# Five gate blocks per batch with one matmul less, the mirror made by ScalarE, VectorE and POOL

## The chip, the cores and the metric

The kernel runs on one core of one Trainium2 chip. The time is the device time of the core in microseconds (us), the median of several executions. A ratio between two kernels is the mean time of the one's fast runs over the mean time of the other's fast runs of the same rounds, so it is not quite the ratio of the medians that stand beside it. A verdict of "faster" or "slower" needs a difference of 2%. Engines: PE is TensorE (PEld its weight load), DVE is VectorE, ACT is ScalarE, POOL is GpSimd, SP issues DMAs.

## The reference

```python
X = np.fft.fft(x, axis=1); X = np.fft.fft(X, axis=2)   # x: 8 x 3008 x 256
y = X.real.reshape(24064, 256)
g = y @ w_gate                                          # 256 x 1536
val = y @ w_val                                         # 256 x 1536
out = (gelu(g) * val) @ w_out                           # 1536 x 256, gelu with erf
```

The DFT's real part has a symmetry. The kernel splits each row into an even part E and an odd part O. A row's gate is `X = E·Wg + O·Wg`, and the gate of its mirror row is `E·Wg − O·Wg` (plus a correction, `EB * yw`, because partition 0 of the odd half carries a row that does not change its sign). So one block of work makes two sets of up to 512 rows.

## The kernel before

The batch is cut into 3 chunks of 512, 512 and 481 columns, each into 12 blocks of 128 features: 36 blocks a batch, numbered 0 to 35 here, 288 in all. One block is the work of one (chunk, fc) pair, woven with the previous block's second half and with the second matmul (L2) of the previous chunk. `# ...` marks what is left out.

```python
        def l1_gate(ci, fc):
            def run():
                n, _, E, O, st, fs = cols_of(ci, fc)
                pg = psum("g")                                     # two banks
                mm(pg, n, "g", "E", fs, E, True, False)
                mm(pg, n, "g", "O", fs, O, False, True)
                gl = gelu_tile()
                nc.scalar.activation(gl[:, 0, :n], pg[:, :n], AF.Gelu)
                st["ps"][fc] = [pg, gl]
            return run

        def l1_gate2(ci, fc):                                      # one block later
            def run():
                n, _, _, O, st, fs = cols_of(ci, fc)
                pg, gl = st["ps"][fc][:2]
                mm(pg, n, "g", "M", fs, O, False, True, skip_group_check=True)   # adds -2 O: now E - O
                nc.scalar.activation(_sub(gl, [[-1, n]], TOK + n - 1), pg[:, :n], AF.Gelu)
            return run
        # ... l1_value: E into pv, ve = EB * yw + pv on DVE
        # ... l1_value2: O into pv; h0 = gelu * pv and vv = 2 ve - pv on DVE; h1 = gelu * vv on POOL

    def tp_rows(b, gi):            # after DFT row group gi: copies one row into EB and into partition 0 of EO
        def run():
            n, y = chunk_len[gi], yrow_dram[b % 2]
            o = y.offset + chunk_off[gi]
            nc.sync.dma_start(
                out=_sub(EB_bufs[b], [[1, n]], chunk_off[gi]), in_=ap_replace(y, ap=[[0, 128], [1, n]], offset=o))
            nc.sync.dma_start(
                out=_sub(EO_bufs[b], [[1, n]], HALF + chunk_off[gi], part_num=1),   # HALF = 1505
                in_=ap_replace(y, ap=[[0, 1], [1, n]], offset=o))
        return run
    # ...
        for i, (parts, fc) in enumerate(blocks):       # the order of one block
            parts["G"][fc]()                           # two gate matmuls, gelu
            if before: before[0]["g"][before[1]]()     # previous block: third gate matmul, mirror gelu
            parts["V"][fc]()                           # value, even
            # four L2 matmuls
            for f in pool.pop(i, []): f()              # POOL folds of a later batch
            if before: before[0]["v"][before[1]]()     # previous block: value, odd; products
            # four L2 matmuls
            for f in fill.pop(i, []): f()              # DFT of the next batch, loads, row copies
            before = parts, fc
```

The fill table holds the next batch's first DFT stage (`s1t`), its last stage (`tp_y`, `tp_e`, `tp_o`, evacuated into EO_sb by ACT), the loads of the batch after, and the row copies. An evacuation copies a finished PSUM bank into SBUF, which frees the bank; a fold is one of POOL's sums over the input rows of a later batch, made before its DFT.

## Time and profile before

| | before |
|---|---|
| median time | 630.39 us (629.39 to 630.58, 3 runs) |
| span of the profiled run | 627.0 us, granted clock 0.996 |
| PE busy | 612.3 us, 98% |
| DVE, ACT, POOL busy | 578.3, 428.4, 505.3 us |

From the page of the kernel before: busy time by engine, the granted TensorE clock in 40 slices (9 is 90% or more), the chain of work that ended last, and the group of gate matmuls (count, then busy us and mean ns of one, then idle time of the engine before them and what ended most of it).

```profile
PE 612.3 (98%) x4195; PEld 405.1 (65%) x4243; DVE 578.3 (92%) x941; ACT 428.4 (68%) x842; POOL 505.3 (81%) x510
...
PEclk8999999999999999999999999999999999999999
...
PE 93%; ACT 2%; issue 1%; DVE 1%; DMA 1%; POOL 1%; POOLq 0%; ACTq 0%
...
L660 PE MATMUL ps_g<-EO_sb,W_sb 128*128 128x512 bf16 (+1 forms) x817 | 228.5, 375 | 3.8 <-ACT gelu_sb L685 0.8
```

The timeline of TensorE in one block of the last batch, before. The columns are start and duration in us, engine, line, operation, tiles and forms, and how many instructions were merged.

```profile
551.41 0.81 PE L660 MATMUL ps_g<-EO_sb,W_sb 128*128 128x512 bf16 x2
552.06 0.38 PE L660 MATMUL ps_v<-EO_sb,W_sb 128*128 128x512 bf16 x1
552.27 0.60 PE L749 MATMUL ps_o<-Wo_sb,h_sb 128*128 128x256 bf16 x4
552.71 0.38 PE L660 MATMUL ps_v<-EO_sb,W_sb 128*128 128x512 bf16 x1
552.93 0.60 PE L749 MATMUL ps_o<-Wo_sb,h_sb 128*128 128x256 bf16 x4
553.36 0.38 PE L660 MATMUL ps_g<-EO_sb,W_sb 128*128 128x512 bf16 x1
```

From 551.41 to 553.36 is one block: 1.95 us. The distance of starts, not the duration, is a matmul's price: 552.27 − 552.06 = 0.21 us for 512 columns, although each matmul "takes" 0.38. (The third gate matmul's record is missing here: 0.65 us pass between 551.41 and 552.06, which is three matmuls.) So the kernel is bound by matmul columns, and a matmul removed is worth 0.2165 us if nothing else waits.

### The profile page before, as it was taken

Reading aid. Unit: us, or ns where it says so; the run is one execution under the profiler, and the core shown is the slowest. Engines: PE = TensorE matmul, PEld = TensorE weight load, DVE = VectorE, ACT = ScalarE, POOL = GpSimd, SP = SyncE. Lnnn points to the kernel's source line nnn. Section 1 sums busy time; section 2 is a strip of 40 time slices with the busy share of each in tenths; the row PEclk is TensorE's granted clock in tenths of the full one; section 3 lists DMA queues with packets and bytes.
Section 4 is the critical chain, followed back from the end, with each engine's and each line's share of the span. In section 5 each row is a group of like instructions: output and inputs, shape, how many; then the busy total and the mean of one; then the engine's idle time right before and its main releaser. Section 6 shows DMA issues by size and latency. Waiting matters only on the chain.

```text
span 627.0 us, 12895 instructions
## 1 busy us (share of the span) xinstructions
PE 612.3 (98%) x4195; PEld 405.1 (65%) x4243; DVE 578.3 (92%) x941; ACT 428.4 (68%) x842; POOL 505.3 (81%) x510
## 2 busy tenths in 40 slices
PE   7999999999999999999999999999999999999997
PEld 3456666666666666666666666666666666666666
DVE  8689989999899999999999998999999999999992
ACT  6777677666776677667676677676676666666661
POOL 8399999989897998879997899969988655555651
PEclk8999999999999999999999999999999999999999
DMA  9961754536353353731645335633212322221123
GB/s 177 227 97 31 210 129 116 144 105 159 99 146 101 98 133 79 184 113 46 160 110 135 101 78 127 148 97 98 62 49 63 91 86 55 51 52 39 42 51 81
DMA packets 54217, 65.40 MB, mean 104 GB/s; under 512 B 7831, under 2 KB 49802, under 8 KB 51754
## 3 DMA queue, kind: packets, MB, share of 16 engines
q1 hardware_dynamic: 47222, 49.03, 30.6%
q0 software_dynamic: 6608, 15.29, 11.4%
q8 instruction: 33, 0.54, 0.4%
q10 hardware_dynamic: 320, 0.26, 0.2%
q14 instruction: 34, 0.28, 0.2%
HBM read 39.65 MB, written 30.17 MB: 111 GB/s over the span
## 4 chain that ended last, share of the span: by engine, by line
PE 93%; ACT 2%; issue 1%; DVE 1%; DMA 1%; POOL 1%; POOLq 0%; ACTq 0%
PE ps_o L749 38%; PE ps_g L660 28%; PE ps_v L660 19%; PE ps_dft L546 2%; PE ps_dft L582 2%; PE ps_o L820 1%; DMA Z_sb<-z 1%; PE ps_dft L443 1%; PE ps_dft L612 0%; ACT gelu_sb L676 0%; POOL h_sb L724 0%; POOL eo_sb L224 0%; DMA out_dram<-out_sb 0%; ACT gelu_sb L685 0%; PE ps_dft L749 0%
## 5 line engine op out<-in xcount | busy, mean ns | idle before, releaser
L724 POOL TENSOR_TENSOR h_sb<-gelu_sb,v_sb 128x512 bf16<-128x512 bf16 (+1 forms) x280 | 319.8, 1146 | 93.1 <-DVE v_sb L722 85.9
L749 PE MATMUL ps_o<-Wo_sb,h_sb 128*128 128x256 bf16 (+1 forms) x2232 | 334.9, 273 | 0.9 <-POOL h_sb L724 0.9
L749 PEld LDWEIGHTS <-h_sb 128*128 128x128 bf16 (+1 forms) x2304 | 228.7, 100 | 112.9 <-POOL h_sb L724 2.6
L676 ACT ACTIVATE gelu_sb<-ps_g 128x512 bf16<-128x512 f32 (+1 forms) x288 | 169.4, 588 | 98.6 <-PE ps_g L660 80.9
L660 PE MATMUL ps_g<-EO_sb,W_sb 128*128 128x512 bf16 (+1 forms) x817 | 228.5, 375 | 3.8 <-ACT gelu_sb L685 0.8
L704 DVE SCALAR_TENSOR_TENSOR ve_sb<-EB_sb,yw,ps_v 128x512 f32<-128x512 bf16 (+1 forms) x280 | 206.3, 737 | 25.9 <-PE ps_v L660 25.0
L660 PE MATMUL ps_v<-EO_sb,W_sb 128*128 128x512 bf16 (+1 forms) x575 | 213.7, 375 | 0.7 <-DVE W_sb L451 0.6
L720 DVE TENSOR_TENSOR h_sb<-gelu_sb,ps_v 128x512 bf16<-128x512 bf16 (+1 forms) x280 | 189.9, 678 | 1.1 <-ACT gelu_sb L685 0.7
L660 PEld LDWEIGHTS <-W_sb 128*128 128x128 bf16 x1440 | 137.2, 98 | 81.1 <-issue 1.8
L722 DVE SCALAR_TENSOR_TENSOR v_sb<-ve_sb,ps_v 128x512 f32<-128x512 f32 (+1 forms) x280 | 187.5, 670 | 0.0
L685 ACT ACTIVATE gelu_sb<-ps_g 128x512 bf16<-128x512 f32 (+1 forms) x288 | 168.7, 586 | 0.0
L769 ACT ACTIVATE out_sb<-ps_o 128x512 f32<-128x512 f32 x92 | 55.0, 598 | 35.7 <-PE ps_o L749 35.6
L224 POOL TENSOR_TENSOR eo_sb<-ab_sb 94x512 bf16<-94x512 f32 (+1 forms) x70 | 77.6, 1111 | 0.5
L549 ACT ACTIVATE S_sb<-ps_dft 96x512 bf16<-96x512 f32 x56 | 32.9, 588 | 14.0 <-PE ps_dft L546 13.9
L592 ACT ACTIVATE EO_sb<-ps_dft 128x512 bf16<-128x512 f32 (+1 forms) x44 | 26.0, 590 | 23.3 <-PE ps_dft L582 22.1
L217 POOL TENSOR_TENSOR ab_sb<-x_raw,x_raw 94x508 f32<-94x508 f32 (+1 forms) x30 | 33.0, 1100 | 0.0
L220 POOL TENSOR_TENSOR ab_sb<-x_raw,x_raw 94x508 f32<-94x508 f32 (+1 forms) x30 | 32.9, 1098 | 0.0
L546 PE MATMUL ps_dft<-eo_sb,G 94*96 94x256 bf16 x119 | 22.5, 274 | 0.2 <-POOL eo_sb L224 0.2
L158 POOL DMA_INDIRECT x_raw<-in_x_dram,idx x18 | 17.1, 948 | 2.9 <-issue 1.1
L582 PE MATMUL ps_dft<-TP,Z_sb 128*128 128x128 bf16 (+1 forms) x184 | 17.8, 218 | 0.0
L582 PEld LDWEIGHTS <-Z_sb 128*128 128x128 bf16 x192 | 14.6, 98 | 1.8 <-DVE Z_sb L534 0.6
L546 PEld LDWEIGHTS <-G 94*96 94x96 bf16 x119 | 13.0, 123 | 1.2 <-issue 0.4
(148 smaller groups left out, 166.2 us busy)
## 6 DMA issues: line engine op xcount, KB each, us to landing
out_dram<-out_sb SPq DMA_DIRECT2D x364, 64.0 KB
x_raw<-in_x_dram SPq DMA_DIRECT2D x10, 768.0 KB
Z_sb<-z SPq DMA_DIRECT2D x7, 768.0 KB
z<-S_sb SPq DMA_DIRECT2D x7, 576.0 KB
EB_sb<-yrow SPq DMA_DIRECT2D x14, 128.0 KB
z<-S_sb SPq DMA_DIRECT2D x7, 192.0 KB
x_raw<-in_x_dram SPq DMA_DIRECT2D x2, 640.0 KB
EB_sb<-yrow SPq DMA_DIRECT2D x7, 120.2 KB
```

Source lines behind the costliest of these rows:

```text
L224: eng.tensor_tensor(_sub(eo, [[C, nj], [1, 128]], j0 * C + g * 128), ab(0, 0, [[1, 128]]), ab(1, 0, [[1, 128]]), op=op)
L546: nc.tensor.matmul(ps[:96, q * C : (q + 1) * C], G[:, j, :], _sub(eo, [[1, C]], j * C), start=(j == js[0]), stop=(j == js[-1]))
L582: nc.tensor.matmul(ps[:, o : o + n], st["Z"][:, pair, g * 128 : g * 128 + 128], _sub(TP, [[1, n]], g * 128), start=True, stop=True)
L660: nc.tensor.matmul(ps[:, :n], W[nm, part][:, fs], src, start=start, stop=stop, **kw)
L676: nc.scalar.activation(gl[:, 0, :n], pg[:, :n], AF.Gelu)
L685: nc.scalar.activation(_sub(gl, [[-1, n]], TOK + n - 1), pg[:, :n], AF.Gelu)
L704: nc.vector.scalar_tensor_tensor(ve[:, :n], EB_bufs[b][:, c0 : c0 + n], yw[:, fc : fc + 1], pv[:, :n], op0=ALU.mult, op1=ALU.add)
L720: nc.vector.tensor_tensor(st["h"][:, fc, 0, :n], gl[:, 0, :n], pv[:, :n], op=ALU.mult)
L722: nc.vector.scalar_tensor_tensor(_sub(vv, [[-1, n]], n - 1), ve[:, :n], 2.0, pv[:, :n], op0=ALU.mult, op1=ALU.subtract)
L724: nc.gpsimd.tensor_tensor(st["h"][:, fc, 1, :n], gl[:, 1, :n], vv[:, :n], op=ALU.mult)
L749: nc.tensor.matmul(pso[:m, half], st["h"][:, fc, sign, h0 : h0 + m], Wo_sb[:, fc, :], start=(fc == 0 and not (first and sign)), stop=(fc = ...
L769: nc.scalar.activation(_sub(osb, [[1, 2 * C]], 0, part_num=m), pso[:m, :], AF.Copy)
```

## The change

In blocks 4, 10, 21, 28 and 33 of batches 1 to 6 the third gate matmul goes. The mirror gate is made as `2E + EB*ywg − X` instead: ACT copies 2E out of the bank (e2) before the odd matmul is added, DVE forms `EB*ywg − X`, POOL adds e2. That is 30 matmuls less: 18 of 512 columns and 12 of 481, 6.3 us of TensorE. Two schedule changes go with it: POOL's folds are moved off the chunk ends, and the last DFT stage of batches 3 to 7 is packed into fewer blocks, earlier.

```diff
+    GATE2 = (4, 10, 21, 28, 33)
         def l1_gate(ci, fc):
+                if two_gate(ci, fc):
+                    mm(pg, n, "g", "E", fs, E, True, True)
+                    e2 = e2_tile()
+                    nc.scalar.activation(e2[:, :n], pg[:, :n], AF.Copy, scale=2.0)
+                    st["ps"][fc] = [pg, gelu_tile(), e2]
+                    return
+        def l1_gate_odd(ci, fc):                       # after the first four L2 matmuls
+                mm(pg, n, "g", "O", fs, O, False, True, skip_group_check=True)
+                nc.scalar.activation(gl[:, 0, :n], pg[:, :n], AF.Gelu)
+                d = v_tile()
+                nc.vector.scalar_tensor_tensor(
+                    d[:, :n], EB_bufs[b][:, c0 : c0 + n], ywg[:, fc : fc + 1], pg[:, :n],
+                    op0=ALU.mult, op1=ALU.subtract)
+                nc.gpsimd.tensor_tensor(d[:, :n], e2[:, :n], d[:, :n], op=ALU.add)
         def l1_gate2(ci, fc):                          # one block later, as before
+                if two_gate(ci, fc):
+                    nc.scalar.activation(_sub(gl, [[-1, n]], TOK + n - 1), pg[:, :n], AF.Gelu)   # pg is d here
+                    return
# ... (tiles, ywg made once at block 14, the call of "O" in the loop)
+                slot_of = [s + {NFC - 1: 2, 0: 1}.get(s % NFC, 0) for s in slot_of]          # folds
-            spread(b, items, s + 7, s0 + NS - 3)
+            spread(b, items, s + 7, s0 + NS - 10 if b > 2 else s0 + NS - 3)                   # DFT rows
```

More of the change, by code (lines that the diff above doesn't have):

```diff
@@ L135, in v_tile, with e2_tile @@
         return work([128, TOK], FP32, "v", 4, "v_sb")
+    def e2_tile():
+        return work([128, TOK], FP32, "e2", 1, "e2_sb")
     def osb_tile():
@@ L245 @@
     one_h = const_pool.tile([1, 1], BF16)
-    yw = const_pool.tile([128, NFC], FP32)
+    yw, ywg = (const_pool.tile([128, NFC], FP32, name=f"yw_{i}") for i in "vg")
     NGP = NJ * NK
@@ L477, in make_yw, with make_ywg @@
         return run
+    def make_ywg():
+        fcs = sorted({i % NFC for i in GATE2})
+        ps = psum("dft")
+        for fc in fcs:
+            nc.tensor.matmul(
+                ps[:, fc : fc + 1], W["g", "O"][0:1, fc * 128 : (fc + 1) * 128], one_h, start=True, stop=True)
+        for fc in fcs:
+            nc.scalar.activation(ywg[:, fc : fc + 1], ps[:, fc : fc + 1], AF.Copy, scale=2.0)
     EO_bufs, EB_bufs = {}, {}
@@ L634, in tp_o @@
         return tp_e(b, gi, 1, engine)
+    NS = NG * NFC
+    GATE2 = (4, 10, 21, 28, 33)
     def store(b, gi, sub, sign, osb_half, queue):
@@ L667, in cols_of, with two_gate @@
             return n, c0, E, O, cstate[ci], slice(fc * 128, (fc + 1) * 128)
+        def two_gate(ci, fc):
+            return 0 < b < B - 1 and ci * NFC + fc in GATE2
         def l1_gate(ci, fc):
@@ L678, in l1_gate, with run @@
             return run
+        def l1_gate_odd(ci, fc):
+            def run():
+                if not two_gate(ci, fc):
+                    return
+                n, c0, _, O, st, fs = cols_of(ci, fc)
+                pg, gl, e2 = st["ps"][fc][:3]
+                del st["ps"][fc][2]
+                mm(pg, n, "g", "O", fs, O, False, True, skip_group_check=True)
[5 more added lines that the diff above has]
+                nc.gpsimd.tensor_tensor(d[:, :n], e2[:, :n], d[:, :n], op=ALU.add)
+                st["ps"][fc][0] = d
+            return run
         def l1_gate2(ci, fc):
@@ L683, in run @@
                 pg, gl = st["ps"][fc][:2]
+                if two_gate(ci, fc):
+                    nc.scalar.activation(_sub(gl, [[-1, n]], TOK + n - 1), pg[:, :n], AF.Gelu)
+                    return
                 mm(pg, n, "g", "M", fs, O, False, True, skip_group_check=True)
@@ L777, in ffn_work @@
             parts = {k: [f(ci, fc) for fc in range(NFC)] for k, f in (
-                ("G", l1_gate), ("V", l1_value), ("g", l1_gate2), ("v", l1_value2))}
+                ("G", l1_gate), ("O", l1_gate_odd), ("V", l1_value), ("g", l1_gate2), ("v", l1_value2))}
             subs = [nsub - 1, *range(nsub - 1)] if last(ci) else range(nsub)
@@ L874, in behind_first_gate @@
         tp_y(0, 0)()
-    NS = NG * NFC
     def plan():
@@ L894, in plan @@
             at(fill, s, f)
+        at(fill, 14, make_ywg)
         for i, f in enumerate(early):
@@ L921, in plan @@
                 slot_of = [4, 4, 5, 5, 6, 6, 7, 7, 8, 8, 9, 13, 13, 14, 15, 15, 16, 17, 17, 18]
+            else:
+                slot_of = [s + {NFC - 1: 2, 0: 1}.get(s % NFC, 0) for s in slot_of]
             for s, f in zip(slot_of, ops):
@@ L972, in feed @@
                 two.pop(0)()
+            parts["O"][fc]()
             for f in pool.pop(i, []):
```

## The prediction

> **What bounds the kernel.** TensorE. The page has PE busy 98% of 627.0 us, and the chain of waits is 93% PE. The Trainium skill ("Perfetto Trace Analysis", Identifying the Most-Contended Engine) warns that matmul busy time says little, because matmuls are pipelined, so I took the pitch of matmul starts from the timeline: 0.2165 us for 512 columns, 0.2035 for 481, 0.109 for 256. One F block of 512 columns is 5 x 0.2165 + 8 x 0.109 = 1.954 us, the period seen in the last batch. A middle batch takes 73.9 us, and its column work with the DFT rows leaves under 1 us unexplained (missing matmul records are not stalls). VectorE is close behind: three instructions a block at about 0.60 each, so 1.8 to 1.85 of 1.954 us. ScalarE needs 2 x 0.49 us a block plus evacuations, POOL 1.12 us for the product plus folds of about 1.22.
>
> **What the change does.** In 5 of 36 blocks of batches 1 to 6 (30 blocks) it removes one gate matmul: 3 x 0.2165 + 2 x 0.2035 = 1.06 us a batch, 6.3 us in all. That is the ceiling. It adds per such block one ACT copy (0.49 to 0.60 us), one DVE instruction (about 0.60) and one POOL fp32 sum (about 1.23, like the fp32 folds).
>
> **What comes back as stalls.** The odd matmul accumulates onto the bank that ACT is still copying. From the start of the even matmul: data out about 0.48 us later, copy 0.60, ACT end to PE start 0.05 (seen where ps_o waits for its evacuation): 1.12 us. PE fills 3 x 0.2165 + 4 x 0.109 = 1.085 us meanwhile: a stall of 0.04. But two of the five blocks (local block 9 of chunks 1 and 2) begin just after an output evacuation on ACT, which puts the copy 0.2 us later: about 0.27 lost. In block 21 the moved DFT row (block 20) queues a second evacuation ahead: about 0.5 lost. Estimate: 3 x 0.04 + 0.27 + 0.5 = 0.9 us lost a batch, against 1.06 saved: PE ps_g waiting for ACT e2.
>
> The rest should be absorbed. DVE needs 7 x 0.6 = 4.2 us in two blocks that PE now does in 3.7; it lags 0.5 us and recovers in three or four blocks within three value banks. The mirror gelu waits for POOL's sum: it starts about 3.7 us after the block began, with room until 4.0, so only a fold just before costs about 0.1. "SBUF — State Buffer" (two separate sides) says a VectorE instruction with two SBUF inputs and a GpSimd one exclude each other; the new difference reads one operand from PSUM, so I expect no blocking.
>
> The moved folds and rows remove little: steady stalls were only about 0.2 us a batch (a gate waiting for its bank behind two evacuations). About -1 us for all. The extra ywg start costs 0.2 to 0.5.
>
> **Predicted: 628.0 us, 624.5 to 632.0 (8 in 10)**, ratio 0.996. Faster by over 2%: 0.01; within 2%: 0.96; slower by over 2%: 0.03.
>
> **What would show it.** L660 matmuls into ps_g fall by 30. PE waits on the ACT copy, most in blocks 21 and 33, near zero in 4, 10 and 28. DVE busy rises 18 to 22 us, ACT about 18, POOL about 36; PE still about 97%. A middle batch shortens by 0.1 to 0.6 us.
>
> **What would make it wrong.** If the copies start earlier than I read, the time nears 624. If POOL's sum is late (over 1.4 us, or behind folds), the mirror gelu blocks ACT in order, the gate banks come late, and the time exceeds 631.

## More of the kernel before

One line of the list of waits of before will matter later (engine, tile and line, what it waited for, total us, times, longest):

```profile
ACT EO_sb L592 <- DMA EO_sb<-yrow: 1.1, 2, 0.6
```

## The result, and the profile after

| | before | after |
|---|---|---|
| median time | 630.3 us (629.39 to 630.58, 4 runs: the three above and one more) | 679.29 us (679.19 to 680.5, 4 runs) |
| ratio | | 1.0784, 95% interval 1.0766 to 1.0803 |
| span, clock | 627.0 us, 0.996 | 677.3 us, 0.977 |

The change is 7.8% slower. The page of the kernel after, the same four lines:

```profile
PE 625.0 (92%) x4168; PEld 406.7 (60%) x4216; DVE 587.2 (87%) x971; ACT 448.3 (66%) x875; POOL 541.3 (80%) x540
...
PEclk9999999998979989999899998999999999999999
...
PE 8%; POOL 2%; DVE 1%; ACT 1%; issue 0%; SPq 0%; DMA 0%; POOLq 0%; ACTq 0%
...
L677 PE MATMUL ps_g<-EO_sb,W_sb 128*128 128x512 bf16 (+1 forms) x787 | 229.0, 381 | 23.2 <-ACT gelu_sb L731 18.3
```

The gate matmuls fell by 30, from 817 to 787 records, yet PE's busy time rose by 12.7 us, and the clock row shows 8s and 7s where it had 9s: for stretches the granted clock fell. The chain could not be followed back far this time (its shares add up to little), so it is not used. The list of waits after shows where engines stood; line numbers moved with the edit.

```profile
ACT gelu_sb L728 <- POOL v_sb L719: 34.9, 28, 4.2
...
DVE v_sb L716 <- ACT gelu_sb L714: 21.1, 30, 1.2
PE ps_g L677 <- ACT gelu_sb L731: 18.3, 17, 5.9
ACT EO_sb L605 <- DMA EO_sb<-yrow: 15.3, 3, 5.8
PE ps_o L795 <- ACT out_sb L815: 13.8, 15, 2.2
```

Two stories are in it. The first two lines belong to the new chain (L714 gelu, L716 difference, L719 sum, L728 mirror gelu); in the last, TensorE waits for an output evacuation, which ACT makes late when it stands in that chain. The fourth line is an old wait, 1.1 us before, now 15.3 us in three places, and it is not part of the gate at all: it is the evacuation of the last DFT stage into EO_sb waiting for a row copy. Most of the third line follows from it: 15.6 of the 18.3 us are three waits (4.81, 4.85 and 5.90 us) right behind those three evacuations.

To see where the 50 us arose, I took the length of the blocks in both traces (the distance between the `ve` instructions of neighbouring blocks on DVE; there are 280, the first eight blocks have none) and subtracted. Sums by batch, with blocks that differ by more than 0.9 us:

| batch | longer by, us | where |
|---|---|---|
| 1 | 8.6 | block 4 +1.25, 12 +1.19, 21 +1.31, 28 +0.95, 30 +3.79, 33 +1.04 |
| 2 | 13.8 | 4 +1.06, 6 +4.48, 10 +1.06, 21 +1.62, 27 +5.13, 28 +1.57 |
| 3 | 10.5 | 6 +1.19, 21 +1.54, 27 +5.15, 28 +1.75 |
| 4 | 11.4 | 6 +1.17, 21 +1.54, 27 +6.20, 28 +1.77 |
| 5 | 3.9 | 6 +1.17, 21 +1.54, 28 +0.93 |
| 6 | 3.3 | 21 +1.54, 28 +1.15, 33 +1.04 |

In batch 5, whose last x load is issued in block 7, and in batch 6, which has none, the gate blocks and their neighbours alone cost. The big steps at block 27 come in batches 2 to 4 alone. Here is block 27 of batch 4 in the timeline of after: the row copy is issued, and the evacuation behind it starts 8.3 us later.

```profile
409.80 0.34 SPq L641 DMA_DIRECT2D EO_sb<-yrow  x1
...
418.13 0.57 ACT L605 ACTIVATE EO_sb<-ps_dft 128x481 bf16<-128x481 f32 x1 [5.82 <-DMA EO_sb<-yrow]
418.60 0.57 ACT L702 ACTIVATE gelu_sb<-ps_g 128x481 bf16<-128x481 f32 x1
...
419.68 0.96 PE L677 MATMUL ps_g<-EO_sb,W_sb 128*128 128x481 bf16 x2 [5.90 <-ACT gelu_sb L731]
```

ACT works in order: while it waits for the copy it makes no gelu, so no gate bank comes free, and TensorE stands for 5.90 us. The stretches around it, after (columns: the stretch and its length, then busy us of PE, PEld, DVE, ACT, POOL with instruction counts, then granted clock, DMA share, GB/s):

```profile
405.00:413.00 8.00, 8.00 (x63) 5.31 (x61) 7.65 (x13) 5.64 (x12) 7.65 (x8) 1.00 0.61 141
413.00:419.60 6.60, 0.78 (x7) 0.47 (x5) 1.67 (x3) 1.47 (x3) 3.24 (x4) 0.86 0.75 168
419.60:424.00 4.40, 4.32 (x16) 2.48 (x16) 1.71 (x3) 1.64 (x4) 1.30 (x2) 0.50 0.11 29
424.00:428.00 4.00, 4.00 (x27) 2.62 (x26) 3.63 (x7) 3.61 (x7) 4.00 (x4) 0.93 0.05 11
```

After the wait TensorE is "busy" but makes 16 matmuls in 4.40 us, against 27 in the next 4.00: the clock is 0.50. So a wait like this one is paid for a second time. It is also the larger part of the rise of PE's busy time: in the five half-clock stretches before the run's end PE was busy 24.7 us, and about half of that, 12.3 us, is extra (an estimate from the trace); what else made PE busier was not traced. The Trainium skill ("TensorE: Matmul & The Clock Gate", What's actually happening) says the array falls to half clock after an idle window of about 3.4 us and returns after a busy one; this trace agrees on the two values of the clock, and its half-clock stretches are 3.41 or 6.83 us long, one or two such windows (but for the last, which the run's end cuts). On the word idle, see the last section.

The other half of the story is one gate block, block 10 of batch 4, after. Read it as a chain: copy, odd matmul (second PE line), gelu, difference, sum, mirror gelu.

```profile
375.07 0.60 PE L677 MATMUL ps_g<-EO_sb,W_sb 128*128 128x512 bf16 x2
375.49 0.60 ACT L696 ACTIVATE e_sb<-ps_g 128x512 f32<-128x512 f32 x1 [0.59 <-PE ps_g L677]
...
376.16 0.38 PE L677 MATMUL ps_g<-EO_sb,W_sb 128*128 128x512 bf16 x1
...
376.64 0.60 ACT L714 ACTIVATE gelu_sb<-ps_g 128x512 bf16<-128x512 f32 x1
...
377.27 0.75 DVE L716 SCALAR_TENSOR_TENSOR v_sb<-EB_sb,yw_g,ps_g 128x512 f32<-128x512 bf16 x1 [0.41 <-ACT gelu_sb L714]
...
378.09 1.27 POOL L719 TENSOR_TENSOR v_sb<-e_sb,v_sb 128x512 f32<-128x512 f32 x1 [0.59 <-DVE v_sb L716]
...
379.40 0.63 ACT L728 ACTIVATE gelu_sb<-v_sb 128x512 bf16<-128x512 f32 x1 [0.86 <-POOL v_sb L719]
...
379.94 0.58 ACT L815 ACTIVATE out_sb<-ps_o 97x512 f32<-97x512 f32 x1
```

The copy costs TensorE nothing here: the odd matmul follows at 376.16, 1.09 us after the even one, as the prediction had it. But the difference does not start when the matmul is done. It waits for the gelu, which reads the same PSUM bank, and starts at 377.27. The mirror gelu therefore starts 379.40 − 375.07 = 4.33 us after the first matmul, not 3.7, and ACT was idle for 0.86 us before it. Behind it in ACT's queue stands the output evacuation (379.94), which frees the only ps_o bank.

### The profile page after: what moved, and what is told of

Its sections match the earlier page's. It is cut to its first block, busy times and chain, and to the rows that moved or that the text cites. A ratio compares the mean times of both kernels' runs of the same rounds, so it can differ in the third digit from the quotient of the medians.

```text
span 677.3 us, 12863 instructions
## 1 busy us (share of the span) xinstructions
PE 625.0 (92%) x4168; PEld 406.7 (60%) x4216; DVE 587.2 (87%) x971; ACT 448.3 (66%) x875; POOL 541.3 (80%) x540
## 3 DMA queue, kind: packets, MB, share of 16 engines
q0 software_dynamic: 6608, 15.29, 10.5%
## 5 line engine op out<-in xcount | busy, mean ns | idle before, releaser
L795 PE MATMUL ps_o<-Wo_sb,h_sb 128*128 128x256 bf16 (+1 forms) x2232 | 340.1, 276 | 14.6 <-ACT out_sb L815 13.8
L795 PEld LDWEIGHTS <-h_sb 128*128 128x128 bf16 (+1 forms) x2304 | 231.2, 101 | 137.4 <-issue 25.9
L677 PE MATMUL ps_g<-EO_sb,W_sb 128*128 128x512 bf16 (+1 forms) x787 | 229.0, 381 | 23.2 <-ACT gelu_sb L731 18.3
L750 DVE SCALAR_TENSOR_TENSOR ve_sb<-EB_sb,yw_v,ps_v 128x512 f32<-128x512 bf16 (+1 forms) x280 | 205.6, 734 | 36.1 <-PE ps_v L677 35.5
L677 PE MATMUL ps_v<-EO_sb,W_sb 128*128 128x512 bf16 (+1 forms) x575 | 216.6, 380 | 1.4 <-DVE W_sb L454 0.6
L702 ACT ACTIVATE gelu_sb<-ps_g 128x512 bf16<-128x512 f32 (+1 forms) x258 | 151.8, 588 | 86.4 <-PE ps_g L677 58.4
L677 PEld LDWEIGHTS <-W_sb 128*128 128x128 bf16 x1410 | 135.3, 98 | 101.4 <-issue 28.8
L731 ACT ACTIVATE gelu_sb<-ps_g 128x512 bf16<-128x512 f32 (+1 forms) x258 | 151.4, 587 | 0.0
L719 POOL TENSOR_TENSOR v_sb<-e_sb,v_sb 128x512 f32<-128x512 f32 (+1 forms) x30 | 37.4, 1246 | 23.0 <-DVE v_sb L716 23.0
L605 ACT ACTIVATE EO_sb<-ps_dft 128x512 bf16<-128x512 f32 (+1 forms) x44 | 25.8, 587 | 27.9 <-DMA EO_sb<-yrow 15.3
L728 ACT ACTIVATE gelu_sb<-v_sb 128x512 bf16<-128x512 f32 (+1 forms) x30 | 18.6, 619 | 34.9 <-POOL v_sb L719 34.9
L716 DVE SCALAR_TENSOR_TENSOR v_sb<-EB_sb,yw_g,ps_g 128x512 f32<-128x512 bf16 (+1 forms) x30 | 22.1, 736 | 21.1 <-ACT gelu_sb L714 21.1
L696 ACT ACTIVATE e_sb<-ps_g 128x512 f32<-128x512 f32 (+1 forms) x30 | 17.6, 587 | 9.4 <-PE ps_g L677 9.4
```

Of the source, the lines that this page charges most:

```text
L677: nc.tensor.matmul(ps[:, :n], W[nm, part][:, fs], src, start=start, stop=stop, **kw)
L719: nc.gpsimd.tensor_tensor(d[:, :n], e2[:, :n], d[:, :n], op=ALU.add)
L750: nc.vector.scalar_tensor_tensor(ve[:, :n], EB_bufs[b][:, c0 : c0 + n], yw[:, fc : fc + 1], pv[:, :n], op0=ALU.mult, op1=ALU.add)
L795: nc.tensor.matmul(pso[:m, half], st["h"][:, fc, sign, h0 : h0 + m], Wo_sb[:, fc, :], start=(fc == 0 and not (first and sign)), stop=(fc = ...
```

## The experiments

Thirteen kernels ran; all gave correct results. Each set was timed against the kernel before on its own chip.

Theory A: two separate causes. (1) The gate chain ends later than predicted, and ACT, in order, holds back the evacuation and the next gate bank. (2) The packed DFT rows bring an evacuation behind a row copy that lands late. Theory B: the schedule is harmless and everything comes from the gate blocks. Theory C (for the gate alone): VectorE has no room for 30 more instructions.

### e1_schedule_only

```diff
-    GATE2 = (4, 10, 21, 28, 33)
+    GATE2 = ()                      # and no ywg; folds and rows as in the change
```

> The moved folds and the earlier rows, with no two-pass block. Theory A (the loss has two separate parts: the chain copy - odd matmul - gelu - difference - sum - mirror gelu in 30 blocks, and the evacuation of the last DFT row, which waits for the row copy that now lands late behind the x loads): 642 to 648 us, with the waits of ScalarE's EO_sb for the EO_sb<-yrow copy still about 15 us in three places. Theory B (the schedule alone is harmless; all comes from the two-pass blocks): 629 to 631 us.

Measured: 659.04 us (654.12 to 659.6) against 629.81, ratio 1.0438 (1.0393 to 1.0483). Theory B is out. Theory A had the kind right and the size too small: 29 us, not 12 to 18. Its list of waits has

```profile
ACT EO_sb L605 <- DMA EO_sb<-yrow: 18.8, 4, 6.1
```

and around the one of batch 2 (stretches, columns as above)

```profile
234.50:241.50 7.00, 2.05 (x16) 1.26 (x14) 2.76 (x5) 0.85 (x2) 4.35 (x5) 0.96 0.90 211
241.50:247.80 6.30, 5.03 (x18) 2.74 (x18) 1.94 (x3) 2.85 (x6) 2.85 (x3) 0.50 0.07 21
```

so the half clock comes on top: blocks 27 and 28 of batch 2 are together 8.6 us longer (6.96 + 1.64) for a wait of at most 6.1. Batches 5 and 6 are 0.10 and 0.13 us longer: with the same packed rows, but no x load near the row copies, there is no cost.

### e2_rows_back

```diff
-            spread(b, items, s + 7, s0 + NS - 10 if b > 2 else s0 + NS - 3)
+            spread(b, items, s + 7, s0 + NS - 3)
```

> The change with the DFT rows spread as before (up to NS - 3), folds still moved, two-pass blocks kept. Theory A: about 17 us less than the changed kernel, 659 to 665 us, and the waits of EO_sb for EO_sb<-yrow under 2 us. Theory B: 676 us or more.

Measured: 660.01 us (658.34 to 661.59), ratio 1.0488 (1.0465 to 1.0511). As theory A has it: 19 us go with one number. (Packed rows with the folds in their old place were not run. The blocks of the x loads hang on those of the folds, but they hardly moved: the loads ahead of the late copy are issued in blocks 24 and 25 in both kernels.)

### e3_gates_only

```diff
-                slot_of = [s + {NFC - 1: 2, 0: 1}.get(s % NFC, 0) for s in slot_of]
+                pass                # folds as before; rows as before too
```

> The two-pass blocks alone: folds and rows where they were before. Theory A: 630 + 6 x 3.3 us, plus a few us where POOL's sum comes late behind folds: 650 to 657 us. Theory B: 675 us or more. If the folds moved off the chunk ends help the two-pass blocks, this one is slower than e2_rows_back; if they hurt (bunched folds delay POOL's sum), it is faster.

Measured: 653.43 us (651.95 to 655.38), ratio 1.0372 (1.0339 to 1.0404). The gate blocks alone cost about 24 us. What is left of TensorE's waits for the output evacuation is

```profile
PE ps_o L795 <- ACT out_sb L815: 9.1, 16, 2.2
```

The gate blocks are 7 us faster with the folds where they were (e2): the moved folds are bunched, and POOL's sum waits in the queue behind them. In e2 block 30 of batch 1 and block 6 of batch 2 are 3.15 and 3.85 us longer than before, in e3 0.85 and 2.51. A part of that is again the half clock: after the start e2 has two such stretches of 3.41 us, e3 one.

### e4_rows_padded

Everything in the change stays, but the odd half of EO_sb starts at an even element.

```diff
-        return work([128, 2, HALF], BF16, "EO", 2, "EO_sb")
+        return work([128, 2, 1536], BF16, "EO", 2, "EO_sb")
-            dst = _sub(EO_bufs[b], [[1, n]], g * HALF + chunk_off[gi])
+            dst = _sub(EO_bufs[b], [[1, n]], g * 1536 + chunk_off[gi])
-                out=_sub(EO_bufs[b], [[1, n]], HALF + chunk_off[gi], part_num=1),
+                out=_sub(EO_bufs[b], [[1, n]], 1536 + chunk_off[gi], part_num=1),
```

> The changed kernel whole, but the odd half of EO_sb begins at element 1536 instead of 1505, so that a row copy and the next evacuation no longer touch neighbouring odd elements; the 14 waits of EO_sb evacuations for a DMA are gone from the program, and nothing else moves. Theory A: the three waits of 5 to 6 us at block 27 of batches 2 to 4 vanish, 660 to 665 us. If it is the late landing itself that holds the kernel, or the row copies' traffic, it stays at 677 us or more.

Measured: 661.22 us (658.16 to 661.84), ratio 1.0488 (1.0453 to 1.0523). So the wait did not protect anything the program needed: the row copy of the first chunk ends at element 2016, counted from the tile's start, the next evacuation begins at 2017, and with 1505 as the start of the half each such pair was ordered. With 1536 the next chunk begins at an even element (2048), the 14 waits (two a batch) are gone from the trace, and 18 us from the time. (That the ordering is by a unit larger than one 2-byte element is an inference from this; which unit was not tried.)

The next three separate the parts of the gate chain.

### e5_difference_first

Two-pass blocks alone, as e3, with the two readers of the bank in the other order.

```diff
                 mm(pg, n, "g", "O", fs, O, False, True, skip_group_check=True)
-                nc.scalar.activation(gl[:, 0, :n], pg[:, :n], AF.Gelu)
                 d = v_tile()
                 nc.vector.scalar_tensor_tensor(d[:, :n], ..., pg[:, :n], ...)
+                nc.scalar.activation(gl[:, 0, :n], pg[:, :n], AF.Gelu)
                 nc.gpsimd.tensor_tensor(d[:, :n], e2[:, :n], d[:, :n], op=ALU.add)
```

> Two-pass blocks alone (as e3_gates_only), but the VectorE difference is issued before the gelu of the same PSUM bank, so the difference waits for the matmul and the gelu waits for the difference. Theory A (the mirror gelu comes about 0.6 us later than predicted because two readers of one bank run one after the other, and ScalarE, in order, then holds up the output evacuation and the next gate bank): the mirror gelu starts about 0.6 us earlier after its block's first matmul, and the time falls from 653 to 641-648 us. Theory C (VectorE simply lacks the time for 30 more instructions): no change, 651 to 655 us.

Measured: 644.48 us (643.17 to 646.7), ratio 1.0236 (1.0207 to 1.0264): 9 us gained by the order of two instructions, where theory C had no change. By the distances of `ve`, 29 of the 30 gate blocks are 0.50 to 0.62 us shorter than in e3. But the new order also spares VectorE its own wait behind the gelu, so a VectorE short of time is not ruled out by this run alone; e6 does that. The same block 10 of batch 4 in this kernel's timeline:

```profile
353.98 0.60 ACT L696 ACTIVATE e_sb<-ps_g 128x512 f32<-128x512 f32 x1 [0.59 <-PE ps_g L677]
...
355.26 0.74 DVE L715 SCALAR_TENSOR_TENSOR v_sb<-EB_sb,yw_g,ps_g 128x512 f32<-128x512 bf16 x1
...
356.03 0.60 ACT L718 ACTIVATE gelu_sb<-ps_g 128x512 bf16<-128x512 f32 x1 [0.97 <-DVE v_sb L715]
356.14 1.28 POOL L719 TENSOR_TENSOR v_sb<-e_sb,v_sb 128x512 f32<-128x512 f32 x1 [0.15 <-DVE v_sb L715]
...
357.48 0.63 ACT L728 ACTIVATE gelu_sb<-v_sb 128x512 bf16<-128x512 f32 x1
```

Now the gelu waits for the difference. From the copy's start, the difference starts after 1.13 us (median of the 30 blocks) instead of 1.75 in e3, and the mirror gelu after 3.55 instead of 3.89, only half of the 0.6 us expected. POOL's sum lasts 1246 ns in both.

### e6_mirror_deferred

Two-pass blocks alone, readers in the order of the change; the mirror gelu of such a block and its product on POOL go one block later.

```diff
             if before:
                 before[0]["g"][before[1]]()
+            if before2:
+                before2[0]["m"][before2[1]]()      # mirror gelu of the block before the previous one
             parts["V"][fc]()
 ...
+            if before2:
+                before2[0]["p"][before2[1]]()      # its product on POOL
             if before:
                 before[0]["v"][before[1]]()
```

> Two-pass blocks alone (as e3_gates_only), with the mirror gelu of such a block and its product issued one block later, so that ScalarE has other work while POOL sums. Order of the two readers of the bank as in the change. Theory A: TensorE's waits for the output evacuation (9 us in e3) and for the mirror gelu nearly vanish; 637 to 645 us. Theory C: 651 to 655 us.

Measured: 637.33 us (636.34 to 637.56), ratio 1.0116 (1.0099 to 1.0133), at the fast edge of what theory A expected. The mirror gelu now starts 5.6 us after the copy (median), against 3.9 in e3, and still the kernel is 16 us faster than e3. What hurt was not that the mirror was late, but that ACT stood still for it. Theory C is out: VectorE has the same 30 instructions and still waits for the gelu before each (the difference starts 1.75 us after the copy, as in e3). TensorE's waits for the evacuation (9.1 us in e3) are gone from the list; waits for POOL's products remain.

### e7_both

Both edits together.

> Both edits, two-pass blocks alone. Theory A: no slower than the better of the two, 636 to 643 us; what remains above 624 is the wait for POOL's products at chunk ends and the copy. Theory C: 651 to 655 us.

Measured: 634.56 us (632.81 to 635.85), ratio 1.0083 (1.0067 to 1.01). Slightly better than the expected range. Taking batch 5 apart by the starts of its matmuls, three things stand against the 1.06 us saved: about 0.25 us each at blocks 21, 28 and 33, where an evacuation on ACT comes just ahead of the copy (at 28 the odd matmul waits for the copy; at 21 and 33 about 0.2 us of it is the second matmul waiting for that evacuation itself), and 1.5 us at block 2, where the next chunk's second matmul waits for POOL's products.

### e8_before_padded

The kernel before with the padding of e4.

> The kernel before, with the odd half of EO_sb beginning at 1536: the waits of evacuations for the row copies go. They were 1.1 us on ScalarE in the profile before and never reached TensorE for more than that, so 0 to 1 us faster: 628.8 to 630.5 us, the same within noise.

Measured: 628.82 us (628.13 to 631.6) against 629.92, ratio 1.0 (0.9975 to 1.0025). The same. In the kernel before the wait was in the program, but all copies except two had landed by then (1.1 us in all).

### e9_other_blocks

e7_both with the padding, and other blocks.

```diff
-    GATE2 = (4, 10, 21, 28, 33)
+    GATE2 = (4, 10, 16, 25, 31)
```

> As e7_both, with EO_sb padded, and the five blocks chosen so that ScalarE has neither an output evacuation nor a DFT evacuation just before the copy: 4, 10, 16, 25, 31 instead of 4, 10, 21, 28, 33. In e7 the copy cost 0.25 us of TensorE at each of 21, 28 and 33, and the wait for POOL's products cost 1.5 us at block 2 of the next batch, after 33. If theory A is the whole of it, about 0.2 us a batch is lost to copies instead of 0.9 and the wait at block 2 shrinks: 625 to 629 us. If 30 blocks cost something else, it stays at 633 us or more.

Measured: 630.59 us (629.62 to 631.82), ratio 1.0013 (0.9998 to 1.0028). Slower than expected, by 1.6 us. The copies cost less, but block 2 of batches 3 to 5 is still 1.37 us longer than before: it was not block 33 that made POOL late, but POOL's folds together with the sums.

### e10_other_blocks_folds

e9 with the folds moved off the chunk ends, as in the change.

> As e9_other_blocks, with the folds moved off the chunk ends as in the change. If the moved folds do what they are meant to (POOL's products ready when the next chunk's second matmuls need them), block 2 waits for nothing: 623 to 627 us, and 1 to 3 us less than e9. If bunched folds only move the wait, no difference from e9 within 1 us.

Measured: 629.67 us (629.18 to 629.93), ratio 0.9999 (0.9985 to 1.0013). A miss: 0.9 us less than e9, so the second branch of the expectation, in which the wait only moves. Block 2 no longer waits, but another wait came up:

```profile
PE ps_dft L559 <- POOL eo_sb L227: 4.2, 7, 1.3
```

The first DFT stage waits for folds that POOL now finishes later. Batch 6, which has no folds after its block 8, is 1.14 us shorter than before: there the 1.06 us of the prediction arrive in full. Batches 1 to 3 are 0.05 to 0.98 us longer than before, 4 and 5 are 0.37 us shorter.

### e11_schedule_padded

e1_schedule_only with the padding.

> As e1_schedule_only (no two-pass block, folds and rows moved, 659 us), with EO_sb padded: no evacuation waits for a row copy any more. If that wait, and the half clock that follows each of its 6 us, are the whole cost of the schedule: 628.5 to 631 us. If the moved folds or the closer rows cost anything by themselves, 633 us or more.

Measured: 629.5 us (628.18 to 630.23), ratio 0.9991 (0.9971 to 1.001). The whole 29 us of the schedule were the waits for the row copies and the half clock after them.

### e12_later_rows and e13_control

e12 is e10 with the first DFT stage one block later after its folds, and the ywg row made at a quieter place. e13 is its control with `GATE2 = ()`.

```diff
-                ready = slot_of[piece * per + per - 1] + 2
+                ready = slot_of[piece * per + per - 1] + (3 if b > 1 else 2)
-        at(fill, 14, make_ywg)
+        at(fill, 22, make_ywg)
```

> As e10_other_blocks_folds, with the first DFT stage of each piece one block later after its folds (3 blocks instead of 2, batches 2 to 7), and the small ywg row made at block 22 of batch 0 instead of 14. In e10 TensorE waited 4.2 us, seven times, for POOL's folds before that stage, only in batches with folds, and 0.8 us for the ywg copies. If POOL's 30 extra sums are what ate the gain of e10: 624.5 to 627 us, ratio to before 0.990 to 0.995. If not: 629 to 630 us.

> As e12_later_rows without any two-pass block (and no ywg): the padding, moved folds and later DFT stage alone. It should be the same as before, 628.5 to 630.5 us; whatever e12 gains over it belongs to the two-pass blocks (5 a batch, at most 6.3 us).

Measured: e12 627.13 us (626.13 to 628.97), ratio 0.9959 (0.9943 to 0.9976), just above the range expected. e13 628.49 us (626.72 to 630.22), ratio 0.9975 (0.9956 to 0.9994). e12 is the fastest median of all, 0.4% below before. The intervals of e12 and e13 overlap, so how much of it is due to the two-pass blocks is not settled; the medians say 1.4 us of a possible 6.3. TensorE's wait for the folds is gone from e12's list, and waits for POOL's products at chunk ends (1.7 us in three places) are back.

## Why the prediction was wrong

The prediction said 628.0 us and "within 2%"; 679.29 came.

- **TensorE bound, 6.3 us the ceiling: right.** Batch 6 of e10 gives 1.14 us against 1.06 predicted for a batch.
- **The copy as a stall on the odd matmul: right in kind and nearly in size.** The free copy costs nothing visible in block 10 (1.09 us from matmul to matmul). In block 21 of the change the odd matmul follows after 1.60 us in batches 2 to 6, 0.5 us later, as predicted. In e7 about 0.25 us went at 21, 28 and 33. I had missed that block 28 has a DFT evacuation ahead of it when the rows are spread as before.
- **"The rest should be absorbed ... it starts about 3.7 us after the block began, with room until 4.0": this step failed.** The sum, of which the prediction gives no terms, fits only if the difference starts when the odd matmul ends: in block 10 the measured 4.33 us less the 0.63 between the starts of gelu and difference (376.64 and 377.27) is 3.70. The difference starts when the gelu of the same bank ends, so the mirror gelu came at about 4.3 us, past the room. With that, ACT stands still, and the evacuation and the next gate bank are late: e3 shows 24 us for the gate blocks as a whole (6.1 us of it are TensorE's waits for POOL's products), e5 gives back 9 by the order of the two readers alone, and e6 16 by giving ACT other work. The Trainium skill says as much as was needed ("PSUM — Partial Sum Buffer", PSUM bank collisions raise a hardware error): no two engines may touch one bank and partition quadrant at once, reads against reads included. I looked up the rule for two readers of SBUF and not the one for two readers of PSUM. The trace agrees in that the two readers never run at once: in all 30 blocks DVE waited for ACT (21.1 us after), and in e5 ACT for DVE (26.2 us).
- **The prediction named the effect, but mostly for another trigger.** It said that a POOL sum that is too long, or behind folds, would block ACT and exceed 631 us. POOL's sum lasted 1246 ns against 1.23 us predicted; its start was what came late. In 23 of the 30 blocks it started within 0.3 us of the difference's end, so there the lateness came from ahead of it. In six it came 1.2 to 3.2 us after, behind POOL's other work; the two worst, block 28 of batch 1 (2.99 us) and block 4 of batch 2 (3.19), stood behind a fold and a product, as the prediction had warned, and two of the five half-clock stretches follow them.
- **"The moved folds and rows remove little ... About -1 us for all": this step failed by more.** They cost 29 us by themselves (e1), all of it at evacuations that wait for a row copy (e11). The wait stood in the list of the kernel before at 1.1 us, and I read it as harmless. Packing the rows put a copy 1 us behind the x loads (in block 25; in batch 4 before, block 28) and the evacuation two blocks behind the copy (before, three). The Trainium skill ("DMA: Bandwidth & Descriptors", Queues, rings and completion order) says that on each DMA engine the descriptors of one ring are consumed in order, and SP issues both the forward loads and the row copies; the 8.3 us from issue to the end of the wait agree with a copy that has to let a load pass first. That the x loads make the copy late is supported by the batches without loads (0.10 and 0.13 us in e1); moving the loads was not tried. Nor is the load on SP's queue told apart from the indirect one on POOL's, issued 1.6 us before that copy and landed at 419.45, 1.3 us after the wait's end.
- **The half clock was not in the sum.** In the change, five waits that left TensorE idle in more than half of a window were followed by stretches at 0.50.
- **Loads of the engines.** ACT rose by 20 us and POOL by 36, as predicted (18 and 36). DVE's busy time rose by only 9 us, but it counts overlapping records once: the lengths of its instructions add up to 641.4 us against 621.4, 20 more, as predicted (18 to 22). PE was to stay at about 97% and came to 92%. The exclusion of VectorE and GpSimd that the prediction cites is not shown by any run: no VectorE instruction of these blocks has two inputs in SBUF, and the difference lasted 736 ns, like `ve` of the same form (734).
- **The two causes do not quite add:** 29 us (schedule) and 24 us (gates) make 53 against 49 for the whole.

## What to carry to other kernels

Before moving work to other engines, write the new chain out with every reader of a PSUM bank in it, and ask what the in-order engine at its end cannot do while it waits; an instruction that is late is cheap, an engine that stands still for it is not. A wait of 1 us in the profile of before that hangs on a DMA is a schedule constraint: look at it before moving the two ends closer together, and check whether the data really overlap, for padding a tile may remove it. Count a long TensorE wait together with the half-clock stretch that follows it.

## What the Trainium skill lacked or had wrong

- "TensorE: Matmul & The Clock Gate" (Why this matters for your kernels) advises against TensorE gaps over about 3 us. Here shorter ones sufficed: in the change TensorE waited 2.13 us (to 165.90), with 1.38 us busy in the 3.40 us before 165.1, and the clock was about 0.50 from 165.1 to 172.0. What counts seems to be how little work a window holds, not one unbroken gap. Cut into windows of 3.41 us from one change of the clock to the next, the 15 traces fit that (PE's busy share is modelled): PE was busy 0 to 49% of the window before each fall (in the change 0, 0, 17, 37 and 40%), and of the windows at full clock without a fall the two least busy had 49% (e6) and 50% (the change). The wait and the stretches of the kernel after (columns as above):

```profile
165.90 1.01 PE L795 MATMUL ps_o<-Wo_sb,h_sb 128*128 128x256 bf16 x4 [2.13 <-ACT out_sb L815]
...
161.70:165.10 3.40, 1.38 (x10) 0.68 (x8) 2.43 (x4) 0.34 (x1) 3.40 (x4) 1.00 1.07 258
165.10:168.50 3.40, 2.60 (x11) 1.46 (x11) 1.08 (x2) 2.72 (x7) 3.40 (x5) 0.50 0.58 137
168.50:172.00 3.50, 3.50 (x13) 1.83 (x13) 0.93 (x3) 1.80 (x4) 2.00 (x2) 0.51 0.34 76
172.00:175.40 3.40, 3.32 (x27) 2.17 (x25) 3.10 (x6) 2.38 (x5) 2.11 (x2) 1.00 0.00 0
```

- "PSUM — Partial Sum Buffer" gives the rule for two engines on one bank, but not what it costs in time: the difference started 1.75 us after the copy behind the gelu and 1.13 us in front of it, worth 9 us over 30 blocks (e3 against e5).
- "DMA: Bandwidth & Descriptors" gives about 2 us as the fixed cost of a transfer in its fit for DMAs that GpSimd issues, and the order within a ring, but no figure for a small copy issued behind a large load: here the row copy issued at 409.80, about 1 us after the x loads, was waited for until 418.13, 8.3 us.
- No page that I read says that two writes to neighbouring elements of a tile may be ordered after each other, worth 18 us here (e4 against the change).
